# Two spectral and two dense layers on one core: the last two tiles of the first dense layer copied straight into the next layer's input, its last product in two column halves, and 38 idle products instead of 24

## The chip, the cores and the metric

The kernel runs on one core of a Trainium2 chip. The metric is device time in microseconds, the median of the runs of a kernel. The profile comes from one of these runs. Engines are named as the profile names them: PE (matrix products), PEld (loads of the stationary operand), DVE (vector), ACT (scalar and activation), POOL and SP. POOL, ACT and SP also issue DMA transfers, each on a queue of its own (q0, q10 and q1).

## The reference

`x` is 2048 tokens of 1024 features in bfloat16. Two kinds of layers are applied twice, each to a normalised `x` and added to `x`:

```
def _A_ref(x, w_r, w_i):                 # spectral filter
    X = rfft2(x.astype(float32)) * (w_r + 1j * w_i)
    return irfft2(X, s=(S, D)).astype(bfloat16)
def _B_ref(x, w1, b1, w2):               # dense, F = 3584
    h = x @ w1 + b1
    return (h * tanh(softplus(h))) @ w2  # mish
x = x + A(layernorm(x)); x = x + B(layernorm(x))
x = x + A(layernorm(x)); x = x + B(layernorm(x))
```

## The kernel before, in words

The four layers run one after another: `layer_A(0)`, `layer_B(0)`, `layer_A(1)`, `layer_B(1)`. The 2048 tokens are 16 tiles of 128, kept in `XS` (tile j in `XS[:, j, :]`). Both dense products use Winograd's form of a 2x2 block product with seven instead of eight block products. The order on every engine is the order in which the program records operations (`op`, `group`, `dma`); each engine runs its own list in order, and a semaphore wait is put in wherever one list needs another's result. A wait therefore holds up everything behind it on its engine or queue. Matrix products are recorded in groups, and one line (L1268 for the second dense product, L635 for the first step of the spectral layer) stands for all of them.

**The end of the first dense layer.** `products(1, ...)` computes the second dense product for tiles 8 to 15 in seven stages (`BACK`) of four token tiles t each. One `tile_product` is 14 products of 128x512 into one PSUM bank. Two sets of four banks alternate: `sets[0]` is banks 6, 7, 0, 1 and `sets[1]` is 2, 3, 4, 5. Stage 3 (`T2`) leaves its sum in `sets[1]`; stage 6 (`T4`) adds to those banks and yields the left 512 columns of tiles 12 to 15. `out` (L1319, DVE) adds bank, accumulator and `XS` into `XS`. `after` holds what is done with each stage's result. The accumulators `P1`, `X7` and `W` are float32 blocks of four tiles.

From stage 5 on, `extra` normalises each tile as soon as its left half is there: `stats_second` (DVE L562, then the aggregate L565), `root` (ACT L444, DVE L446), `apply` (DVE L524, into a ring of four buffers). The statistics of the right half were taken in stage 3.

**The way into the next layer.** The spectral layer's first step, `s1`, wants the tokens turned: `XR` has one partition per pair of tile and 128-column block, `row_of(j, h)`, and holds there 128 tokens x 128 features. A tile gets there in one of two ways. `xn_store` writes it to DRAM (`xn_scratch`, on POOL) and `xr_load` (on SP) reads it back as eight rows of 32 KB. `xr_direct` copies it from the ring buffer straight into the eight rows, one DMA per row and part. Tiles 0 to 14 go by DRAM; tile 15 goes directly in two parts of 64 tokens, that is 16 DMAs of 16 KB dealt over POOL, ACT and SP in turn. SP's list at this point is the loads of tiles 8 to 14, then its five direct copies; POOL's is the stores of tiles 8 to 14, six direct copies, and then the loads of the next layer's tables.

`s1` has 16 groups of eight products. Group j reads tokens 8j to 8j+7 of every tile, so groups 0 to 7 need the first half of all tiles and groups 8 to 15 the second half (`r_xr`). Each group fills a pair of banks, of which there are four, and is copied out by ACT (L641, groups 1, 3, 5, 7, 8, 9, 11, 13, 15) or DVE (L643). After `products` the kernel records `spin(24, 7)`: 24 products of 128x512 (L652) whose result in bank 7 nobody reads.

Of the kernel before, what the change touches and what calls it, by code (L numbers as in the profile page):

```python
# [6 lines left out]
ALU = mybir.AluOpType  # L7
P = 128
# [172 lines left out]
class KB:  # L181
# [375 lines left out]
    def stats_second(self, j, h, first):  # L557

        r = self.r_mv[j]
        if first:  # L560
            r.begin()
        self.op(self.dve, lambda e: e.bn_stats(self.BN[:, j, 6 * h:6 * h + 6], self.XS[:, j, 512 * h:512 * h + 512]),  # L562
                reads=[self.r_xs[j]], parts=[r])
        if not first:
            self.op(self.dve, lambda e: e.bn_aggr(self.MV[:, j, :], self.BN[:, j, :]), reads=[r], writes=[r])  # L565

    def pair(self):
        i = self.npair % 4
# [516 lines left out]
    def layer_B(self, li, last):  # L1085
        pe, dve, act, sp, pool = self.pe, self.dve, self.act, self.sp, self.pool
        PS, PSb, NF = self.PS, self.PSb, self.NF
# [174 lines left out]
            self.dma(pool, self.w2s_d[T_OF[name]][:, 7 * k:7 * k + 7, :], dst.ap, f"w2t{n}{k}", reads=[dst.res],  # L1262
                     writes=[self.r_w2d[T_OF[name]][k]])

        def tile_product(n, t, bank, ap, part, start):

            for k in range(2):
                self.group([lambda e, i=i, k=k, b=PB[n][k].ap: e.matmul(  # L1268
                    PS[:, bank, :], ap[:, i, t * P:(t + 1) * P], b[:, i - 7 * k, :],
                    start=(start and i == 0), stop=(i == 13), skip_group_check=True) for i in range(7 * k, 7 * k + 7)],  # L1270
                    reads=part(k) + [PB[n][k].res], writes=[self.r_bank[bank]])

# [3 lines left out]
        def products(p, s_off, stages, extra, loads=True):  # L1276
# [10 lines left out]
            ap = {"A11": AT[0][0].ap, "A12": AT[0][1].ap, "A21": AT[1][0].ap, "A22": AT[1][1].ap, "S": S.ap}  # L1287
# [10 lines left out]
            sets = ((6, 7, 0, 1), (2, 3, 4, 5))  # L1298
# [10 lines left out]
            def add(dst, bank, name, t):  # L1309
                (d, rd), (a, r) = acc(dst), acc(name)  # L1310
                self.op(dve, lambda e: e.tensor_tensor(d[t], PS[:, bank, :], a[t], ALU.add), reads=[self.r_bank[bank], r[t]], writes=[rd[t]])  # L1311

            def out(bank, name, t, i, h):
                x, rx = xs_of(i, t, h)
                a, reads = x, [self.r_bank[bank]]
                if name:
                    a, reads = acc(name)[0][t], reads + [acc(name)[1][t]]
                done = Res("done")
                self.op(dve, lambda e: e.tensor_tensor(x, PS[:, bank, :], a, ALU.add), reads=reads, writes=[rx, done])  # L1319
                if last:  # L1320
                    j = 4 * c[i] + t
                    self.dma(sp, self.out[0, j * P:(j + 1) * P, 512 * h:512 * h + 512], x, "st", reads=[done])
                elif stages is BACK and h:
                    self.stats_second(4 * c[i] + t, 1, True)

            def after(b, t, bank):

                if b == "B11":
                    a, r = acc("P1")
                    self.copy(act, a[t], PS[:, bank, :], [self.r_bank[bank]], [r[t]])  # L1330
                elif b == "B21" and stages is STD:
                    out(bank, None, t, 0, 0)
                elif b == "B21":
                    out(bank, "P1", t, 0, 0)
                elif b == "T3":
                    add("X7", bank, "P1", t)
                elif b == "T1":
                    add("W", bank, "X7", t)
                    fold("W", t, 1, 1)
                    if stages is BACK:  # L1340
                        fold("X7", t, 1, 0)
                elif b == "T2":
                    out(bank, "W", t, 1, 1)
                    add("W", bank, "P1", t)
                elif b == "B22":
                    fold("W", t, 0, 1)
                    out(bank, "W", t, 0, 1)
                    fold(*(("P1", t, 0, 0) if stages is BACK else ("X7", t, 1, 0)))
                else:
                    out(bank, "X7", t, 1, 0)  # L1350
# [6 lines left out]
            for n, (a, b, g, start) in enumerate(stages):  # L1357
                for t in range(4):
                    bank = sets[g][t]
                    if n or t:  # L1360
                        tile_product(n, t, bank, ap[a], lambda k: part(a, k), start)
                    after(b, t, bank)
                    for f, k in sums.get((n, t), ()):
                        f(k)
                    if t == 3 and n < 5 and loads:
                        for k in range(2):
                            load_b(stages, n + 2, k)
                    extra(n, t)
# [166 lines left out]
        def extra(n, t):  # L1535
            if n == 0:
                self.stats_act(12 + t)
            if not last:
                own_sums(n, t)
            if (n, t) == (1, 3):  # L1540
                self.sums_to_mv(12, 4)
                self.scales(12, 4)
                normal(12)
                for j in (13, 14, 15):
                    xn[j] = self.apply(j)
            if (n, t) == (2, 2):
                for j in (13, 14, 15):
                    transposed(3, j - 12, xn[j], act, (6, 7, 0)[j - 13])
            turn(2)
            if (n, t) == (4, 3) and not last:  # L1550
                ws[2:] = self.open_slots("WS", self.ob["WS"], 2)
                self.fill_slot(ws[2], 2)
            if n == 6 and not last:
                self.stats_act(t)
            if (n, t) == (5, 3):
                ws[0:2] = self.open_slots("WS", self.ob["WS"], 0, 1)
                for i in range(2):
                    self.fill_slot(ws[i], i)
                token_sums(1, last=False)
            if (n, t) == (6, 1):  # L1560
                B.update(token_sums(1))
# [26 lines left out]
        def extra(n, t):  # L1588
            if last:
                return  # L1590
            if (n, t) == (2, 0):
                self.warm(ACT.Sqrt)
            if (n, t) == (3, 3):
                self.open_xr()
                for j in range(8):
                    self.xr_load(j)
            if n >= 5:
                j = 4 * n - 12 + t
                self.stats_second(j, 0, False)
                self.root(j, 1)  # L1600
                b = self.apply(j, out=True)
                if j < 15:
                    self.xn_store(j, b)
                if j > 8:
                    self.xr_load(j - 1)
                if j == 15:
                    self.xr_direct(j, b, 2, (pool, act, sp))
        products(1, self.ob["XT2"], stages, extra)
        if not last:
            self.spin(24, 7)  # L1610


def build_kernel(nc, A_x, A_w_r, A_w_i, B_x, B_w1, B_b1, B_w2, out):
# [35 lines left out]
```

## Time and profile before

| what | value |
|---|---|
| median of 5 runs | 937.39 us (936.89 to 939.92) |
| profiled execution | 937.39 us, of which the span is 935.6 us |
| PE, share of the span busy | 94% |
| DVE, ACT, POOL | 66%, 46%, 17% |
| mean granted TensorE clock | 0.987 |
| last product of tile 15 read by DVE | 478.82 us |
| idle products | 478.62 to 483.96 us |
| first product of `s1` in the second spectral layer | 489.67 us |
| last copy out of `s1` ended | 501.04 us |

Times within the run count from the start of the span. A row of the timeline gives start, duration, engine, line, operation, output and inputs, and in brackets how long the engine had been idle and what ended that. Rows on SPq and ACTq are issues of DMAs; the transfer lands later. In the chain of waits every piece is what the next one waited for. "PEclk" in the table of windows is the granted clock as a part of full speed.

### The profile page before, as it was taken

The numbers are of one execution on the slowest core, as the hardware profiler recorded it, in microseconds if no ns is written. First come the engines' busy times: TensorE is split into PE (matmuls) and PEld (weight loads), VectorE is DVE, ScalarE is ACT, GpSimd is POOL, SyncE is SP. The second block draws the span as 40 slices with busy tenths as digits, with TensorE's granted clock in tenths as the row PEclk, the third lists the DMA queues.
The fourth block names the chain that finished last, engine by engine and source line by source line (L and its number), as shares of the span: only waits on it lengthen the run. The fifth ranks groups of instructions, "written<-read, shape, count | busy, mean of one in ns | idle before, by whom it ended". The sixth has DMA issues, their size and how long they took to land.

```text
span 935.6 us, 13481 instructions
## 1 busy us (share of the span) xinstructions
PE 876.5 (94%) x5473; PEld 472.1 (50%) x5473; DVE 618.9 (66%) x973; ACT 427.5 (46%) x623; POOL 159.1 (17%) x183
## 2 busy tenths in 40 slices
PE   0799799999999999999979987999999999999998
PEld 0577486444444444444437765754444444444443
DVE  7698368686889667568746865647746665554473
ACT  7798475456203475410008975745551015553000
POOL 3922003960004641010130200000000000000000
PEclk9999989999999999999999998999999999999999
DMA  9969854674786388364640798433155635832432
GB/s 287 259 232 300 202 134 122 216 277 142 262 262 243 138 311 292 115 243 143 251 147 32 221 228 200 159 118 119 54 185 177 209 113 190 282 118 74 175 125 112
DMA packets 146335, 174.68 MB, mean 187 GB/s; under 512 B 66248, under 2 KB 125736, under 8 KB 146152
## 3 DMA queue, kind: packets, MB, share of 16 engines
q1 hardware_dynamic: 133424, 127.48, 44.4%
q0 software_dynamic: 10672, 44.67, 13.3%
q10 hardware_dynamic: 2176, 1.66, 0.6%
q8 instruction: 43, 0.70, 0.3%
q14 instruction: 20, 0.16, 0.0%
HBM read 130.00 MB, written 40.89 MB: 183 GB/s over the span
## 4 chain that ended last, share of the span: by engine, by line
PE 81%; DMA 6%; DVE 5%; POOL 2%; ACT 2%; SPq 2%; issue 1%; DVEq 0%; POOLq 0%; ACTq 0%
PE PS L1268 35%; PE PS L1186 26%; PE PS L1148 9%; POOL ARENA L1081 2%; SPq L251 2%; PE PS L799 2%; PE PS L725 2%; PE PS L1020 2%; PE PS L824 2%; DMA ARENA<-in_B_w_dram 1%; PE PS L1109 1%; DMA ARENA<-in_A_x_dram 1%; DMA ARENA<-c_bt 1%; DMA ARENA<-u_scratch 1%; DMA u_scratch<-ARENA 1%
## 5 line engine op out<-in xcount | busy, mean ns | idle before, releaser
L1268 PE MATMUL PS<-ARENA 128*128 128x512 bf16 x1568 | 340.1, 379 | 0.0
L1186 PE MATMUL PS<-ARENA 128*128 128x512 f16 (+1 forms) x1232 | 267.8, 379 | 0.6 <-POOL ARENA L1081 0.5
L1268 PEld LDWEIGHTS PS<-ARENA 128*128 128x128 bf16 x1568 | 153.3, 98 | 184.6
L1191 DVE TENSOR_TENSOR ARENA<-PS,ARENA 128x512 f32<-128x512 f32 x220 | 151.8, 691 | 95.9 <-PE PS L1186 91.1
L1186 PEld LDWEIGHTS PS<-ARENA 128*128 128x128 bf16 x1232 | 120.2, 98 | 146.9 <-POOL ARENA L1081 2.5
L1196 ACT ACTIVATE ARENA<-ARENA,B 128x512 bf16<-128x512 f32 x132 | 95.1, 721 | 66.9 <-DVE ARENA L1191 60.8
L574 ACT ACTIVATE ARENA<-PS 128x512 f32<-128x512 f32 (+2 forms) x82 | 61.1, 745 | 119.4 <-PE PS L1186 96.4
L1148 PE MATMUL PS<-ARENA 128*128 128x256 bf16 (+1 forms) x576 | 87.4, 310 | 0.1
L1081 POOL TENSOR_TENSOR ARENA<-ARENA 128x512 bf16<-128x512 bf16 x56 | 71.3, 1273 | 74.7 <-DVE ARENA L524 60.1
L453 ACT ACTIVATE ARENA<-XS 128x1024 bf16<-128x1024 bf16 x52 | 54.8, 1053 | 36.9 <-DVE XS L1319 33.0
L1148 PEld LDWEIGHTS PS<-ARENA 128*128 128x128 bf16 x576 | 55.7, 99 | 26.7 <-DVE ARENA L1114 0.7
L1293 DVE TENSOR_TENSOR ARENA<-ARENA 128x3584 bf16<-128x3584 bf16 x32 | 63.9, 2017 | 0.0
L1319 DVE TENSOR_TENSOR XS<-PS,ARENA 128x512 bf16<-128x512 f32 x52 | 35.7, 689 | 39.0 <-PE PS L1268 38.7
L1152 ACT ACTIVATE ARENA<-PS,B 128x256 bf16<-128x256 f32 (+1 forms) x72 | 38.4, 541 | 35.8 <-PE PS L1148 35.3
L1311 DVE TENSOR_TENSOR ARENA<-PS,ARENA 128x512 f32<-128x512 f32 x48 | 32.9, 688 | 28.9 <-PE PS L1268 28.4
L1196 ACT ACTIVATE ARENA<-PS,B 128x512 bf16<-128x512 f32 x44 | 30.2, 685 | 18.0 <-PE PS L1186 18.0
L1307 DVE TENSOR_TENSOR ARENA<-ARENA,XS 128x512 f32<-128x512 f32 x52 | 36.7, 731 | 0.5
L1163 DVE TENSOR_TENSOR ARENA<-ARENA 128x2048 f16<-128x2048 bf16 x16 | 25.3, 1580 | 17.6 <-PE PS L1148 17.3
L799 PE MATMUL PS<-ARENA 128*128 128x256 bf16 x256 | 32.4, 273 | 3.9 <-DVE ARENA L788 3.2
L781 DVE TENSOR_TENSOR ARENA<-ARENA 128x1024 bf16<-128x1024 bf16 x32 | 22.0, 687 | 21.0 <-ACT ARENA L777 21.0
L472 DVE BATCH_NORM_STATS2 BN<-XS 128x6 f32<-128x512 bf16 x52 | 32.7, 671 | 4.6 <-DMA XS<-in_A_x_dram 4.6
L444 ACT ACTIVATE RS<-MV,EPS 128x1 f32<-128x1 f32 (+2 forms) x11 | 3.3, 296 | 70.7 <-DVE MV L565 70.0
(97 smaller groups left out, 832.5 us busy)
## 6 DMA issues: line engine op xcount, KB each, us to landing
ARENA<-in_B_w_dram SPq DMA_DIRECT2D x30, 896.0 KB, 6.5
ARENA<-w1s_scratch SPq DMA_DIRECT2D x30, 896.0 KB, 4.7
ARENA<-w2s_scratch SPq DMA_DIRECT2D x24, 896.0 KB, 6.6
ARENA<-in_B_w_dram SPq DMA_DIRECT2D x26, 512.0 KB, 5.3
w1s_scratch<-ARENA POOLq DMA_DIRECT2D x14, 896.0 KB, 4.2
u_scratch<-ARENA SPq DMA_DIRECT2D x14, 512.0 KB, 3.5
ARENA<-u_scratch SPq DMA_DIRECT2D x14, 512.0 KB, 5.9
w2s_scratch<-ARENA POOLq DMA_DIRECT2D x8, 896.0 KB, 4.2
```

The costliest lines, as they stand in the source:

```text
L453: self.op(act, lambda e, i=i, f=f: e.activation(junk.ap, x, f, accum_out=sums[:, i:i + 1]), reads=[self.r_xs[j]], writes=[junk.res], parts ...
L574: fn = (lambda e: e.activation(dst, src, ACT.Copy)) if scale is None else \
L799: fns.append(lambda e, c=c, part=part: e.matmul(ps[:, c * 256:(c + 1) * 256], yk.ap[:, part, c * P:(c + 1) * P], t[:, (128, 0)[part]:(384, ...
L1081: self.op(self.pool, lambda e, dst=A(dst), x=A(x), y=A(y), op=op: e.tensor_tensor(dst, x, y, op), reads=[b.res] + list(after), writes=[b.rs])
L1148: fns.append(lambda e, db=db, bank=bank, fl=fl: e.matmul(PS[:, bank, 0:w], wb.ap[:, db, fl * P:(fl + 1) * P], x.ap[:, db, tok], start=(db ...
L1152: self.op(act, lambda e, bank=bank, ft=ft, at=at: e.activation(at[:, tok], PS[:, bank, 0:w], ACT.Mish, bias=self.B1[:, ft:ft + 1]), reads= ...
L1186: self.group([lambda e, db=db: e.matmul(PS[:, bank, :], A[:, db, :], mov[:, db, :], start=(start and db == 0), stop=(db == 3), skip_group_ ...
L1191: self.op(dve, lambda e: e.tensor_tensor(dst.ap, PS[:, bank, :], x.ap, ALU.add), reads=[self.r_bank[bank], x.res], writes=[dst.res])
L1196: self.op(act, lambda e: e.activation(at, src, ACT.Mish, bias=self.B1[:, ft:ft + 1]), reads=[res, self.r_b1], writes=[ra])
L1268: self.group([lambda e, i=i, k=k, b=PB[n][k].ap: e.matmul(PS[:, bank, :], ap[:, i, t * P:(t + 1) * P], b[:, i - 7 * k, :], start=(start an ...
L1293: self.op(dve, lambda e: e.tensor_tensor(ap[dst][:, f, :], ap[x][:, f, :], ap[y][:, f, :], op), reads=part(x, k) + part(y, k), writes=part ...
L1307: self.op(dve, lambda e: e.tensor_tensor(a[t], a[t], x, ALU.add), reads=[rx], writes=[r[t]])
```

## The change

Tile 14 also goes directly, in one part: eight DMAs of 128 tokens x 128 features (32 KB), dealt alternately over POOL and SP; its store to DRAM and its load are gone, and the load of tile 13 stands on SP after SP's four copies. The 16 DMAs of tile 15 are dealt over the queues by a written list (ACT six, POOL six, SP four). The last product, stage 6 of tile 15, is computed as two halves of 256 columns. The left half goes on in its own bank; the right half starts anew in bank 1, and for that stage 3 adds its sum in these columns into `X7` beforehand. Each half is added into `XS` and gets its own statistics (`stats_columns`, four pieces of 256 columns and an aggregate over them, in the `BN` space of tiles 0 and 1). The idle products become 38.

```diff
+    def stats_columns(self, j, u):
+        r = self.r_mv[j]
+        if u == 0:
+            r.begin()
+        bn = self.BN[:, 0:2, :].rearrange("p a b -> p (a b)")
+        a = (512, 768, 0, 256)[u]
+        self.op(self.dve, lambda e: e.bn_stats(bn[:, 6 * u:6 * u + 6], self.XS[:, j, a:a + 256]), reads=[self.r_xs[j]],
+                writes=self.r_mv[0:2], parts=[r])
+        if u == 3:
+            self.op(self.dve, lambda e: e.bn_aggr(self.MV[:, j, :], bn), reads=[r] + self.r_mv[0:2], writes=[r])
...
-        def tile_product(n, t, bank, ap, part, start):
+        def tile_product(n, t, bank, ap, part, start, d=slice(0, 512)):
...
-                    PS[:, bank, :], ap[:, i, t * P:(t + 1) * P], b[:, i - 7 * k, :],
+                    PS[:, bank, d], ap[:, i, t * P:(t + 1) * P], b[:, i - 7 * k, d],
...
-            def out(bank, name, t, i, h):
+            def out(bank, name, t, i, h, d=slice(0, 512)):
...
+                elif stages is BACK and h and (i, t) == (1, 3):
+                    for u in range(2):
+                        self.stats_columns(15, u)
...
                 elif b == "T2":
                     out(bank, "W", t, 1, 1)
                     add("W", bank, "P1", t)
+                    if stages is BACK and t == 3:
+                        x7, r7 = acc("X7")
+                        self.op(dve, lambda e: e.tensor_tensor(x7[t][:, 256:512], PS[:, bank, 256:512], x7[t][:, 256:512], ALU.add),
+                                reads=[self.r_bank[bank]], writes=[r7[t]])
...
+                    if stages is BACK and (n, t) == (6, 3):
+                        for u, at in enumerate((bank, sets[0][t])):
+                            d = slice(256 * u, 256 * u + 256)
+                            tile_product(n, t, at, ap[a], lambda k: part(a, k), bool(u), d)
+                            out(at, "X7", t, 1, 0, d)
+                            self.stats_columns(15, 2 + u)
+                        extra(n, t)
+                        continue
...
-                self.stats_second(j, 0, False)
+                if j < 15:
+                    self.stats_second(j, 0, False)
                 self.root(j, 1)
                 b = self.apply(j, out=True)
-                if j < 15:
+                if j < 14:
                     self.xn_store(j, b)
-                if j > 8:
-                    self.xr_load(j - 1)
-                if j == 15:
-                    self.xr_direct(j, b, 2, (pool, act, sp))
+                    if j > 8:
+                        self.xr_load(j - 1)
+                elif j == 14:
+                    self.xr_direct(j, b, 1, (pool, sp))
+                    self.xr_load(13)
+                else:
+                    self.xr_direct(j, b, 2, (act, pool, sp, act, pool, act, pool, sp) * 2)
         products(1, self.ob["XT2"], stages, extra)
         if not last:
-            self.spin(24, 7)
+            self.spin(38, 7)
```

## The prediction

> **What bounds the kernel now**
>
> I read the page, the list of PE's waits, the chain of waits around the edited seam, the timeline there, the table of windows, and the DMA queues in short windows. PE is busy for 94% of the span, so the question is where it is not. PE's waits (what it waited for, total us, times, longest):
>
> ```profile
> PE PS L595 <- DVE ARENA L592: 21.2, 1, 21.2
> PE PS L1020 <- DMA ARENA<-u_scratch: 6.2, 4, 2.0
> PE PS L635 <- DMA ARENA<-ARENA: 5.7, 1, 5.7
> ```
>
> The first is the start of the kernel. The third is the longest single wait for a transfer, and the one place that the change touches. The chain of waits through it (start, us, what):
>
> ```profile
> 478.02 0.56 DVE ARENA L524
> 478.58 0.66 issue
> 479.24 2.84 DMA xn_scratch<-ARENA
> 482.08 0.02 issue
> 482.09 0.60 SPq L251
> 482.69 0.04 issue
> 482.74 0.54 SPq L251
> 483.28 0.04 issue
> 483.32 6.11 DMA ARENA<-ARENA
> 489.43 0.24 issue
> 489.67 4.82 PE PS L635 x48
> 494.49 0.02 issue
> 494.51 6.53 ACT ARENA L641 x7
> ```
>
> Tile 14 is normalised until 478.57, goes to DRAM and lands at 482.08. Only then can SP load it back, and SP's direct copies of tile 15 stand behind that load. The timeline shows that tile 15 itself was ready at 481.59, and that ACT and POOL began at once:
>
> ```profile
> 478.62 5.34 PE L652 MATMUL PS<-BD 128*128 128x512 bf16 x24
> 478.82 0.69 DVE L1319 TENSOR_TENSOR XS<-PS,ARENA 128x512 bf16<-128x512 f32 x1 [0.25 <-PE PS L1268]
> 481.04 0.55 DVE L524 TENSOR_SCALAR ARENA<-XS,MV,RS 128x1024 bf16<-128x1024 bf16 x1
> 481.62 3.35 ACTq L251 DMA_DIRECT2D ARENA<-ARENA  x5
> 482.74 3.17 SPq L251 DMA_DIRECT2D ARENA<-ARENA  x5
> ```
>
> The windows (length, busy PE, PEld, DVE, ACT, POOL, then PEclk, DMA share, GB/s) show a second loss. The idle products end at 483.96, the clock halves about 3.1 us later and stays half for 6.6 us:
>
> ```profile
> 487.10:489.60 2.50, 0.00 (x0) 0.00 (x0) 0.00 (x0) 0.00 (x0) 0.00 (x0) 0.50 0.48 76
> 489.60:493.70 4.10, 4.03 (x39) 4.06 (x40) 2.45 (x2) 1.44 (x2) 0.00 (x0) 0.50 0.00 0
> ```
>
> At half clock PE sets the pace of s1: its first copies out start 0.85 us apart (490.72, 491.58, 492.43, 493.28). From 494.51 ACT copies without a gap, so there ACT does.
>
> Why do SP's copies take up to 6 us? SP's queue in the 0.1 us from 482.70, when the load of tile 13 moves (packets, MB, share of 16 engines):
>
> ```profile
> q1 hardware_dynamic: 8, 0.26, 1024.5%
> ```
>
> Eight packets of 32 KB take 10.245 x 1.6 = 16.4 us of engine time, or 2.05 us each on eight engines. Load 14 then runs from about 484.5 on the same eight, and whatever is queued there waits: the last 40 packets of SP's direct copies move at 488.1 to 489.4. I read these two as one cause; the trace does not name the engines.
>
> **The change, part by part**
>
> *Tile 14 directly.* Removed: POOL's store of tile 14 (0.89 us of issue, 2.84 to landing) and SP's reload (0.60 of issue, eight packets of 2 us). Added: eight copies of 32 KB, four on POOL at about 0.54 us and four on SP at about 0.60 (the medians of the direct copies' issue). SP starts at 478.6 and is through by 481.1. The reload of tile 13 now stands behind these four, but it waits anyway for its store, which landed so that it issued at 481.33. So SP is free at about 481.9 for tile 15, against 482.74. POOL is through by about 481.4, before tile 15 is ready. New in flight on the eight slow engines at 480.6 to 481.7 are the direct packets, beside the rest of store 13: 4 copies x 9 packets x about 22 ns (SP's copies at 487 to 488) = 0.8 us at most, so load 13 moves between 482.75 and 483.5 and is done at 484.8 to 485.5. There is no load 14 behind it.
>
> *Order of queues for tile 15.* ACT gets six copies instead of five, SP four instead of five, three ACT, three POOL and two SP in each half. The first half is issued by about 483.7, and needs 1.4 us to its first packets (ACT's issue at 481.62, packets at 483.0). Packets on the eight engines flush after load 13: the eight copies of a half are 8 x 80 packets over 16 engines, 40 each at about 25 ns, so 1 us. The first half and tile 13 are there at 486.0 to 487.2. Copies of the second half leave by 485.8; they gate the ninth group of s1, over 4 us after its start, and cost nothing. POOL's FT table load keeps its place at 485.1.
>
> *More idle products.* 24 took 5.34 us, or 0.2157 us each more. 38 starting at 478.65 end at 487.0. So s1 starts at the later of 487.0 and the data: I take 487.1, **2.57 us earlier than 489.67**. The spin itself may hold it up by up to 1 us; if the data are late it costs nothing.
>
> *Clock.* The wait after the idle products falls from 5.7 us to a few tenths, and the clock should stay full. Then s1 is set by ACT's nine copies (groups 1, 3, 5, 7, 8, 9, 11, 13, 15): a group of eight takes 0.64 us alone (first layer's s1 in the chain of waits), the second is there at about 1.0 us, then 2 x 1.02 + 7 x 0.93 = 8.55, in all 9.6 us. Before, s1 took from 489.67 to 501.04 = 11.37. **Gain 1.77 us.** DVE's seven copies of 1.2 us fit beside it.
> Rule and row: the Trainium skill, "TensorE: Matmul & The Clock Gate" (Terms, and "What's actually happening"), gives one idle window of about 3.4 us to the half clock, and a price of throttled time x (1 - K/N). On the whole 6.6 us this makes 3.3 us and the sum 931.8; but products ran for only 4.0 us of it, which makes 2.0 and 933.1. I keep 1.77, since at full clock the copies take over as the limit.
>
> *Last product in halves.* PE: 28 products of 256 columns at 0.109 us (L1148's eight in 0.87) are 3.05 us for 3.02. The second half goes to a free bank, so PE waits for no read. On DVE the intended gain, a shorter last add and statistics (0.69 + 0.69), is not there: DVE is busy with tile 14 until 478.57, and waits only 0.25 us for the full product today. After that come two adds (estimate 0.42 each[...]) and two statistics (0.413, the 256-column row L484), 1.8 us with gaps against 1.70 now, and an aggregate of 24 values (0.264) instead of 12 (0.209). Tile 15 is ready **0.15 to 0.2 us later**, at 481.77. ACT's first copies move with it, but the spin's end covers that.
>
> *Stage T2.* One more add of 0.42 us and two statistics of 256 for one of 512 (+0.14). Both come with the stage's last tile (add at 443.89), after which DVE idles 0.83 us before the add of 446.00; hidden there, and 0.56 us outright if that gap were gone.
>
> *Later.* Everything behind s1 moves 4.3 us earlier. In the lull of the next stage the clock is half from 572.7 to 579.1. In the first layer the same lull was half for 10 us, and the way from its start to the long products took 24.30 us (114.78 to 139.08) against 23.25 (570.93 to 594.18). Where the clock's window falls is new after the shift: between -0.2 and +1.05 us, I take +0.3.
>
> A rule speaks against the change: the Trainium skill, "DMA: Bandwidth & Descriptors" (Anatomy of one DMA; Bandwidth), gives about 2.0 us fixed per transfer and calls transfers under 64 KB descriptor-dominated. Taken one after another, four of 32 KB on SP are 4 x 2.08 = 8.3 us from 478.6: load 13 would leave at 487, arrive at 491, and s1 would start at about 492, a loss of 2.6 us. The rows say that transfers in one queue overlap: ACT's copies, issued 0.6 to 0.75 us apart, move packets at that same pitch. I go with the rows.
>
> Sum: 2.57 + 1.77 - 0.3 = 4.0 us. The profiled execution took 937.39 us, of which 935.6 is span, and is the median of the five, so the time is **933.3 us**.
>
> **Rivals**
>
> 1. *Data late, clock kept.* Load 13 or a queue is later than I think, and s1 starts between 488 and 490. With idle products until 487.0 the wait stays under 3.1 us. For: store 13 shares engines with the new copies, and landings of up to 6.1 us have been seen. Against: no load 14. Gain 1.77 + (0 to 1.7) - 0.3: 934.2 to 935.9.
> 2. *Small copies clog SP's queue; slower.* SP's four copies of tile 14 stand ahead of load 13 and of SP's part of tile 15. If each 128-row copy held the queue for the 2 us of the rule or more, s1 starts at 492 or later. Past 490.1 (487.0 + 3.1) the clock halves again and the gain of 1.77 is gone too, so this is the point from which it decides. Start at 492 to 494: 2.3 to 4.3 us slower, 939.7 to 941.7. For: ACT's landings are on average 1.5 us apart where issues are 0.7. Against: those landings fall together with the 32 KB packets, and packets elsewhere follow the issues.
> 3. *The seam's gain is given back.* The next lull in the half clock for the longer time (-1.05), and the spin or s1's copies slower than I count: about 935.5 to 937.
>
> **How the numbers follow**
>
> My forecast 0.67, with 932.0 to 934.5 as its own range; rival 1 0.16, rival 2 0.09, rival 3 0.08. A run of this kernel tells 0.2%, 1.87 us, from no change: the borders are 935.52 and 939.26. Faster: 0.67 + 0.12 of rival 1 + 0.03 of rival 3 = 0.82. Slower: 0.08 of rival 2. Same: the rest, 0.10. The range goes from 931.8 (data early, s1 on ACT alone) to 936.2, which leaves out rival 2 and half of rival 3.
>
> **What would show it right or wrong**
>
> In the changed kernel: 38 idle products ending near 487; s1's first product within about 1 us after them; granted clock 1.00 over all of s1; ACT's copies out of s1 without gaps, s1 about 9.6 us long; aggregate of tile 15 at about 480.4 (no gain from the halves); SP's reload of tile 13 still near 481.3 to 482.1; no store and load of tile 14. I am wrong if s1's wait for a direct copy is again over 3 us, if the clock is half at s1's start, or if tile 15 is normalised clearly before 481.5.

## The result and the profile after

| | before | after |
|---|---|---|
| median | 938.35 us (48 runs) | 936.25 us (27 runs, 933.02 to 940.85) |
| ratio | | 0.9981, 95% interval 0.9971 to 0.999 |
| profiled execution | 937.39 us, span 935.6 us | 935.05 us, span 933.2 us |
| mean granted clock in it | 0.987 | 0.993 |

About half of the forecast gain: 2.1 us (938.35 less 936.25) for 4.1 (937.39 less 933.3), and just outside the range, which ended at 936.2. The forecast started from a median of five runs, 937.39; 48 runs of the same kernel gave 938.35. Two further measurements of the unchanged kernel after gave 935.62 and 937.57 us; the interval of the second reaches no change (table below).

The chain of waits of the kernel after through the seam (start, us, what):

```profile
476.86 5.77 DMA xn_scratch<-ARENA
...
482.64 0.66 SPq L251
...
483.90 4.65 DMA ARENA<-ARENA
488.56 0.26 issue
488.82 0.62 PE PS L647 x8
...
492.98 5.61 ACT ARENA L653 x6
```

It is the chain of before, one tile earlier: the store of tile 13, SP's load of tile 13, one of SP's copies of tile 15, `s1`. That last copy took 4.65 us (6.11 before). A queue's copies of one half report to one semaphore, so this is the time until all of SP's first half was reported. PE's wait for it was 1.1 us. The timeline:

```profile
479.36 8.37 PE L664 MATMUL PS<-BD 128*128 128x512 bf16 x38
488.82 6.83 PE L647 MATMUL PS<-M,ARENA 128*128 128x128 bf16 x104 [1.09 <-DMA ARENA<-ARENA]
489.91 8.68 ACT L653 ACTIVATE ARENA<-PS 128x1024 bf16<-128x1024 f32 x9 [8.29 <-PE PS L647]
```

The short wait flatters: the idle products now end at 487.73 instead of 483.96, so most of the old wait lies under them. What counts is `s1`'s first product, at 488.82 against 489.67. ACT's nine copies run without a gap, because the clock stayed full, as the windows show (the columns as before):

```profile
487.10:489.60 2.50, 1.41 (x18) 0.91 (x16) 0.14 (x1) 0.00 (x0) 0.00 (x0) 1.00 0.47 89
489.60:493.70 4.10, 3.97 (x66) 3.48 (x64) 4.10 (x4) 3.68 (x4) 0.00 (x0) 1.00 0.00 0
```

The way up to the seam differs by up to 1.5 us from profile to profile, so seams are compared from DVE's read of tile 14's last product, here called out 14: 475.80 before, 476.50 after. From there `s1` starts at +13.87 before and +12.32 after, and its last copy ends at +25.24 and +22.09. That is 3.15 us in these two profiles: 1.55 in the start, 1.60 in the length of `s1` (11.37 and 9.77). Of it, 0.70 is taken off because this run reached out 14 later (the other two profiles of the same kernel reached it at 475.50 and 475.15, so the change is not the reason), and 2.45 is left, against 2.4 between the spans. From the end of `s1` to the end of the span it is 434.56 us before and 434.61 after: nothing was given back there.

### The profile page after: what moved, and what is told of

Read it like the earlier page. It is cut to its first block, busy times and chain, and to the rows that moved or that the text cites. A ratio compares the mean times of both kernels' runs of the same rounds, so it can differ in the third digit from the quotient of the medians.

```text
span 933.2 us, 13549 instructions
## 1 busy us (share of the span) xinstructions
PE 878.2 (94%) x5501; PEld 472.8 (51%) x5501; DVE 619.7 (66%) x977; ACT 427.6 (46%) x623; POOL 159.8 (17%) x186
## 4 chain that ended last, share of the span: by engine, by line
PE 81%; DMA 6%; DVE 6%; POOL 3%; ACT 2%; issue 1%; SPq 1%; POOLq 0%; DVEq 0%; ACTq 0%
PE PS L1280 34%; PE PS L1198 26%; PE PS L1160 9%; POOL ARENA L1093 2%; PE PS L811 2%; PE PS L737 2%; PE PS L836 2%; PE PS L1032 2%; DMA XS<-in_A_x_dram 1%; DMA ARENA<-in_B_w_dram 1%; PE PS L1121 1%; DMA ARENA<-c_bt 1%; DMA ARENA<-u_scratch 1%; POOL ARENA L251 1%; DVE ARENA L655 1%; DMA u_scratch<-ARENA 1%
## 5 line engine op out<-in xcount | busy, mean ns | idle before, releaser
L1280 PE MATMUL PS<-ARENA 128*128 128x512 bf16 (+1 forms) x1582 | 340.1, 377 | 0.0
L1331 DVE TENSOR_TENSOR XS<-PS,ARENA 128x512 bf16<-128x512 f32 (+1 forms) x53 | 35.8, 679 | 38.2 <-PE PS L1280 38.0
L789 ACT ACTIVATE ARENA<-PS 128x1024 bf16<-128x1024 f32 x32 | 33.4, 1075 | 4.5 <-PE PS L785 4.5
```

The source lines that it names most:

```text
L1280: self.group([lambda e, i=i, k=k, b=PB[n][k].ap: e.matmul(PS[:, bank, d], ap[:, i, t * P:(t + 1) * P], b[:, i - 7 * k, d], start=(start an ...
```

## The experiments

Times in the table count from out 14; "long" is from the first product of `s1` to its last copy; the clock is that during the wait and `s1`. The median of before in the five batches was 937.85, 938.1, 938.46, 938.61 and 938.69 us.

| run | median us | ratio to before [95%] | first product of s1 | PE's wait | s1 long | clock |
|---|---|---|---|---|---|---|
| before (profile) | 938.35 | | +13.87 | 5.7 | 11.37 | half, 7 us |
| after (profile) | 936.25 | 0.9981 [0.9971, 0.999] | +12.32 | 1.1 | 9.77 | full |
| e1_direct14 | 937.88 | 0.9996 [0.9984, 1.0008] | +13.49 | 5.3 | 10.75 | half, 3.5 us |
| e2_spin38 | 937.5 | 0.9988 [0.9977, 0.9999] | +14.46 | 3.3 | 12.12 | half, 7 us |
| e3_nohalves | 937.09 | 0.9985 [0.9972, 0.9997] | +13.53 | 2.3 | 11.02 | half, 3.5 us |
| e4_after | 935.62 | 0.9975 [0.9963, 0.9987] | +13.32 | 2.1 | 9.77 | full |
| e6_direct13 | 937.92 | 0.9998 [0.9988, 1.0007] | +14.71 | 3.5 | 10.76 | half, 3.5 us |
| e7_direct13_spin30 | 938.31 | 1.0003 [0.9992, 1.0014] | +15.14 | 5.6 | 11.34 | half, 7 us |
| e8_ftlate | 936.04 | 0.9981 [0.9973, 0.9989] | +12.73 | 1.5 | 9.77 | full |
| e10_spin44 | 935.69 | 0.9972 [0.9962, 0.9982] | +14.63 | 2.1 | 11.01 | half, 3.5 us |
| e11_no13 | 936.03 | 0.9976 [0.9964, 0.9987] | +12.72 | 3.2 | 12.05 | half, 7 us |
| e12_15only | 931.91 | 0.9935 [0.9923, 0.9947] | +10.18 | 0.7 | 9.77 | full |
| e13_alldirect | 940.43 | 1.002 [1.0007, 1.0033] | +16.39 | 6.5 | 11.46 | half, 7 us |
| e14_alldirect_spin30 | 940.84 | 1.0024 [1.0013, 1.0035] | +17.57 | 8.1 | 11.13 | half, 7 us |
| e15_14and15 | 935.36 | 0.9969 [0.9957, 0.9981] | +12.04 | 2.5 | 11.00 | half, 3.5 us |
| e16_13and15 | 934.94 | 0.9962 [0.9951, 0.9974] | +12.07 | 2.6 | 9.77 | full |
| e17_onepart | 937.06 | 0.999 [0.9978, 1.0001] | +13.64 | 2.4 | 11.03 | half, 3.5 us |
| e18_actstore | 934.67 | 0.9963 [0.995, 0.9975] | +13.13 | 1.9 | 9.76 | full |
| e19_actstore44 | 934.36 | 0.9958 [0.994, 0.9976] | +13.02 | 0.5 | 9.77 | full |
| e20_after | 937.57 | 0.9987 [0.9973, 1.0001] | +14.54 | 3.3 | 9.76 | full |

**The parts of the change.** e1_direct14 is before with tile 14 sent directly and the new dealing of the queues; e2_spin38 is before with more idle products; e3_nohalves has both and lacks the column halves; e4_after is the whole change again.

```diff
+                elif j == 14:                                          # e1, e3
+                    self.xr_direct(j, b, 1, (pool, sp))
+                    self.xr_load(13)
...
-            self.spin(24, 7)
+            self.spin(38, 7)                                           # e2, e3
```

> The kernel before with the direct copies of tile 14 and the new deal of queues alone (24 idle products, no halves). Theory (two gains that need each other): s1 starts about 1.5 us earlier than before counted from DVE's read of tile 14's last product (13.87 us there), since the reload of tile 13 now gates it; the idle products still end 5 us after the last product, PE then waits over 4 us, so the clock is half at s1's start and s1 takes about 11.4 us. Sum: 1.5 us faster, ratio 0.998. Rival (the clock is the whole gain): no change, ratio 1.000. Rival (the idle time is now short enough to keep the clock): 3 us faster.

> The kernel before with 38 idle products alone. Theory: s1 starts 13.9 us after DVE's read of tile 14's last product as before, the wait after the idle products falls from 5.7 to 2.7 us. If the clock halves only after 3.1 us of idling, s1 is at full clock and takes 9.7 instead of 11.4 us: 1.6 us faster, ratio 0.9983. Rival (the clock is judged in fixed windows of about 3.4 us, so it depends on where the wait falls): half of the runs gain, the median moves by under 1 us and the runs spread over 2 us more. Rival (the clock was no part of the gain): ratio 1.000.

> The changed kernel without the column halves: direct copies of tile 14, new deal of queues, 38 idle products. Theory (halves bring nothing, since DVE is busy with tile 14 when the last product ends): same as the changed kernel within 0.2 us, tile 15 normalised 5.8 us after DVE's read of tile 14's last product against 5.9 with halves; ratio to before 0.998. Rival (halves are what brings tile 15 earlier): slower than the changed kernel by 0.5 us.

> The changed kernel once more, for a second profile beside the others on one chip. Theory: from DVE's read of tile 14's last product to the end of s1 it is 22.1 us at full clock, against 25.2 before, so 3.1 us faster at the seam; the median gains less (about 2 us) because in some runs the clock halves at s1 or longer in the lull behind it, which would show as a granted clock under 0.99 in the slow runs. Rival (the direct copies land late in some runs): slow runs with a clock of 0.993 and an s1 that starts over 13 us after that read.

Measured: each part alone is within 0.12% of before. With tile 14 direct and 24 idle products PE still waits 5.3 us and the clock goes; with 38 idle products alone the data come at +14.46, the wait is 3.3 us and the clock goes too. Together they bring 0.15 to 0.25% (e3, e4); these intervals overlap that of e2 (0.9977 to 0.9999), so how the gain divides is not settled by the medians. With e1 the first product came at +13.49, not near the forecast +11.3 nor the 1.5 us expected of this run: the direct way of tile 14 is itself worth only some tenths. The halves cost DVE 0.1 us, as forecast: tile 15 is normalised at +5.90 with them (e4_after) and +5.80 without (e3_nohalves). Their own effect on the time isn't told apart: the intervals of e3_nohalves and e4_after overlap.

**What might hold the copies of tile 15.** e6_direct13 and e7_direct13_spin30 send tile 13 directly as well, so that the last reload is tile 12's; e8_ftlate holds back a table load of POOL (`c_ft`, 192 KB) that moves between the copies; e10_spin44 has 44 idle products.

```diff
+                elif j == 13:                                          # e6, e7
+                    self.xr_direct(j, b, 1, (pool, sp))
+                    self.xr_load(12)
...
+        late = [self.Y.res] if self.li and g == 2 else []              # e8: c_ft waits for s1's result
...
+            self.spin(44, 7)                                           # e10
```

> The changed kernel with tile 13 also copied directly (eight copies of 128 rows, four on POOL and four on SP, before SP's reload of tile 12), still 38 idle products. Theory (the reload of tile 13, with its 32 KB rows on eight DMA engines, holds the direct copies back): data are ready before the idle products end, PE waits under 0.2 us for a transfer, s1 starts 11.3 us after DVE's read of tile 14's last product (12.3 and 13.3 in the two profiles of the changed kernel), the clock stays full in every run: 1 to 2 us faster than the changed kernel, ratio 0.996. Rival (the FT table load on POOL is what holds them back): s1 starts at 12.3 to 13.3 as in the changed kernel, no gain. Rival (more small copies clog SP's queue): s1 later than 13.3, slower than the changed kernel.

> As e6_direct13 with 30 idle products, which end 9.6 us after the same read. Theory: data are ready at 10 to 10.7, so s1 starts there, 0.6 to 1.3 us earlier than in e6_direct13, at full clock; ratio 0.995. Rival (FT table load): s1 at 12.3 to 13.3 after 3 us of idling, the clock halves, ratio 0.999 or more.

> The changed kernel with the third FT table's load (POOL, right behind its direct copies) held until s1 is done, where it still has 4 us before its use. Theory (reload of tile 13): s1's start moves by under 0.3 us. Rival (the table's packets from DRAM delay the last packets of the direct copies on the engines they share): s1 starts 0.8 to 1.5 us earlier, about 11.5 to 12 us after the read, and the median is 1 us or more under the changed kernel's. Both may hold in part: then about 0.5 us.

> The changed kernel with 44 idle products, which end 12.6 us after the read. Theory (in part of the runs the wait between the idle products and s1 lets the clock halve, so the changed kernel's runs spread from 933 to 941): the wait falls under 0.8 us, the slow runs go, the median falls by 1 us or more against the changed kernel and no run has a granted clock under 0.988. Rival (the spread has other causes): same spread, and a median 0 to 0.3 us worse.

Measured: one more direct tile makes the start later, +14.71 and +15.14. Without the table in the way `s1` starts at +12.73, inside the spread of the kernel after (+12.32 to +14.54 in three profiles), and the time is that of after, so the table is at most a small part of it. With 44 idle products the data were late too (+14.63; tile 13's store had needed 7.6 us to land), and the clock was lost in the middle of `s1`; the time, 935.69 us, is within the spread of after, and its runs still reach from 932.2 to 940.2 us, which they were expected not to do.

**Leaving tiles out.** In the next kernels a tile's rows of `XR` are filled early with those of a tile that was stored long before (j - 8), and its own store, load or copies are left out, so the next layer works on that tile's values in its place; 30 idle products make the landing visible as PE's wait. e11_no13 leaves out tile 13, e12_15only tiles 13 and 14. e13_alldirect, and e14_alldirect_spin30 with 30 idle products, are complete kernels with tiles 8 to 15 direct.

```diff
+                self.xr_load(13, 5)                                    # e11, e12, e15: rows of tile 13 from tile 5
+                self.xr_load(14, 6)                                    # e12, e16: rows of tile 14 from tile 6
+                self.xr_load(12, 4)                                    # e15: rows of tile 12 from tile 4
...
-                if j < 14:                                             # e13, e14
-                    self.xn_store(j, b)
-                    if j > 8:
-                        self.xr_load(j - 1)
-                elif j == 14:
+                if j < 15:
+                    b.unread = False
                     self.xr_direct(j, b, 1, (pool, sp))
-                    self.xr_load(13)
```

> The kernel after with tile 13's store and reload left out of the seam: its rows of s1's input are filled early from tile 5's (so tile 13's values in the output are tile 5's in effect), and 30 idle products instead of 38 (end near 485.3). Times are counted from the read of tile 14's last product (out 14). Theory A (the store, reload and eight 32 KB rows of tile 13 pin s1's start, because the copies of tile 15 queue behind them on SP and on eight DMA engines): s1 starts at +10.0 to +11.3 and the clock stays full, 934.0 to 935.0. Rival B (the small copies of tiles 14 and 15 land late by themselves): s1 starts at +12.3 to +13.5, as in the kernel after, with 2 to 3 us of waiting, 935.5 to 937.

> As the kernel without tile 13 at the seam, and tile 14's direct copies left out too (its rows filled early from tile 6's), so that only tile 15's sixteen copies remain at the end; 30 idle products. Theory A: little more to gain, s1 at +9.7 to +10.8, within 0.8 us of the kernel without tile 13. Rival B1 (tile 14's eight copies delay tile 15's): s1 over 1 us earlier than without tile 13 alone. Rival B2 (tile 15's own copies take 5 us to land after they are issued): s1 still at +12 or later, so nothing gained by leaving out either.

> The kernel after with tiles 8 to 13 also sent directly (eight copies each, POOL and SP in turn), so no store, no reload and no 32 KB row in the last eight tiles; 38 idle products as before. Theory A: every tile's copies are through before the next one is ready, so s1 starts at the end of the idle products, about +11.0 to +11.6, clock full, 934.3 to 935.5. Rival B (small copies are slow to land and pile up: 48 more of them, and POOL or SP fall behind): s1 at +12.3 to +15, 935.6 to 938.

> The same with 30 idle products, which end near 485.3 at +9.6, so that the landing of tile 15's first half itself is seen as PE's wait. Theory A: s1 at +10 to +11.3 with a wait under 1.5 us, 933.8 to 935.3. Rival B: s1 no earlier than with 38, a wait of 3 us or more and the clock at half in part of s1, 936.5 to 938.

Measured: without tile 13 little or nothing is gained (+12.72), which spoke against my reading, that the 32 KB rows are the cause. Without tile 14 as well `s1` starts at +10.18 and the time falls to 931.91 us. The chain of waits of e12_15only:

```profile
482.25 0.86 ACTq L251
483.11 0.03 issue
483.14 2.30 DMA ARENA<-ARENA
485.44 0.49 issue
485.92 0.62 PE PS L648 x8
```

This is what tile 15 needs when tiles 13 and 14 are out of the way: 2.3 us from issue to landing, half of the 4.65 in the kernel after. All tiles direct is slower than before. The table of DMAs of e12_15only and then of e13_alldirect (output and input, queue, count, size, median us from issue to landing):

```profile
ARENA<-ARENA ACTq DMA_DIRECT2D x6, 16.0 KB, 2.4
ARENA<-ARENA POOLq DMA_DIRECT2D x6, 16.0 KB, 2.1
ARENA<-ARENA SPq DMA_DIRECT2D x4, 16.0 KB, 2.2
```

```profile
ARENA<-ARENA ACTq DMA_DIRECT2D x6, 16.0 KB, 6.5
ARENA<-ARENA POOLq DMA_DIRECT2D x6, 16.0 KB, 6.0
ARENA<-ARENA SPq DMA_DIRECT2D x4, 16.0 KB, 7.1
```

The windows of e13_alldirect point to why (the last three columns are the clock, the mean share of 16 DMA engines, GB/s):

```profile
480.00:484.00 4.00, 4.00 (x20) 1.84 (x19) 2.58 (x7) 0.29 (x1) 2.82 (x7) 1.00 1.22 68
484.00:488.00 4.00, 3.08 (x15) 1.18 (x12) 0.00 (x0) 0.00 (x0) 3.15 (x6) 1.00 1.54 64
```

The engines have packets open all the time (the shares add up to over 1, so packets overlap in this count), and still only 64 to 68 GB/s move. A tile of 262,144 bytes needs 3.9 to 4.1 us at that pace, and a tile is ready every 3.02 us (out 14 to the next one, 475.80 to 478.82 before): they pile up, as the rival had it. The time of one packet, from packets and share in one us, first of e12_15only at 483, then of e13_alldirect at 485:

```profile
q10 hardware_dynamic: 160, 0.03, 15.0%
```

```profile
q1 hardware_dynamic: 237, 0.05, 124.7%
```

0.150 x 16 us over 160 packets is 15 ns; 1.247 x 16 over 237 is 84 ns. There the same small packet takes over five times as long. The late copies also hold up DVE, which waits for a buffer that they still read: in e14_alldirect_spin30 tile 15 itself is ready 1.3 us later than in after (+7.15 for +5.90).

**Rows or small copies.** Both suspects were still in e11_no13, since load 12's rows had moved into the place of load 13's. So e15_14and15 leaves out tiles 12 and 13 (no 32 KB row moves near the end), and e16_13and15 leaves out tile 14 only. e17_onepart is the kernel after with tile 15 in eight copies of 128 tokens, e18_actstore has the stores of tiles 8 to 13 on ACT's queue.

```diff
+                    self.xr_direct(j, b, 1, (act, pool, sp, act, pool, act, pool, sp))     # e17, tile 15
...
+        prog, tag = (self.act, "xa") if j >= 8 else (self.pool, "xw")                      # e18, e19: xn_store
```

> The rows of tiles 12 and 13 are left out of the seam (filled early from tiles 4 and 5), so that no 32 KB row moves after about 477; tile 14 and tile 15 go directly, 30 idle products. Counted from out 14. Theory P (the small copies of tile 14 and tile 15 slow each other: packets take 15 ns alone and 30 to 80 when many copies are open): s1 at +12 to +13, as without tile 13, about 935.5 to 936.5. Theory R (32 KB rows of whatever tile comes last hold eight engines for 2 us, and without tile 13 it was load 12's): s1 at +10 to +10.8, as with tile 15 alone, about 932 to 933.5.

> Tile 14 is left out of the seam (its rows filled early from tile 6's), tile 13 still goes by store and reload, tile 15 directly; 30 idle products. Theory P: without tile 14's small copies s1 starts at +10.2 to +11, about 932 to 933.5. Theory R: load 13's rows and SP's queue behind it still hold tile 15's copies, s1 at +12 to +13.5, about 935.5 to 937. Both causes together would show +12 in both of these kernels.

> The kernel after with tile 15 copied in one part (eight copies of 128 rows, issued in half the time) instead of two: half as many copies, but s1's start now needs all of tile 15. 38 idle products. Theory P: the packets are the same and the last of the tile lands as late as it did (c. 489 to 490), so s1 is 0.5 to 1.5 us later than in the kernel after (+13.5 to +14.5) and the clock is lost more often: 936.5 to 938. Rival (the number of copies counts, each with its own fixed cost): s1 at +11.5 to +12.5 and 934.5 to 935.5, better than after.

> The kernel after with the stores of tiles 8 to 13 on ACT's queue (ACT idles for most of this stage) instead of POOL's. Store 13 is issued at once and load 13 needs not wait for 5.5 to 8 us. Theory R: load 13 leaves 0.5 to 2 us earlier, SP's copies of tile 15 with it, s1 at +11.3 to +12.3, 934.5 to 935.5. Theory P: store 13's landing is set by the packets ahead of it on the engines, whichever queue it comes from; s1 stays at +12.3 to +14, 935.5 to 936.5.

Measured: +12.04 and +12.07 where tile 15 alone had +10.18. Each of the two, tile 14's small copies without any 32 KB row, and tile 13's rows without tile 14, costs 1.9 us by itself in these profiles. One profile stands for each, and three of the kernel after lie 2.2 us apart, so the size is rough; that each costs something the medians show: 935.36 and 934.94 us against 931.91, with intervals far apart. The chain of waits of e15_14and15:

```profile
480.76 0.81 ACTq L251
...
481.60 4.23 DMA ARENA<-ARENA
485.83 0.45 issue
```

The same third copy of ACT as in e12_15only, issued just as soon after tile 15, lands after 4.23 instead of 2.30 us. Its packets are not slower and not late. ACT's queue up to 483.25 in e15_14and15 and up to 484.75 in e12_15only, 1.6 us after that copy's issue in both (481.60, 483.14):

```profile
q10 hardware_dynamic: 240, 0.05, 10.4%
```

```profile
q10 hardware_dynamic: 240, 0.05, 6.0%
```

In both all 240 packets of the three copies (480 for the six) have begun by then, at 15 to 16 ns each (0.104 x 16 x 2.25 us and 0.060 x 16 x 3.75 us over 240). The landing comes at 485.83 and 485.44, that is 2.6 and 0.7 us later. So what tile 14's copies delay here is the report of the landing, behind the packets. And of e16_13and15:

```profile
477.25 5.63 DMA xn_scratch<-ARENA
...
482.90 0.60 SPq L251
...
483.55 0.61 SPq L251
...
484.21 4.52 DMA ARENA<-ARENA
488.73 0.24 issue
488.97 0.62 PE PS L648 x8
```

Here SP waits for the store of tile 13 (5.63 us), issues the load, and then its copies of tile 15. SP's queue in the us from 484:

```profile
q1 hardware_dynamic: 8, 0.26, 104.5%
```

1.045 x 16 us over eight packets is 2.1 us each, as before the change. It is not SP's queue alone that they delay. The last copies of the first half on each queue, in e16_13and15:

```profile
ARENA<-ARENA ACTq DMA_DIRECT2D x1, 16.0 KB, 4.5
ARENA<-ARENA SPq DMA_DIRECT2D x1, 16.0 KB, 4.5
ARENA<-ARENA POOLq DMA_DIRECT2D x1, 16.0 KB, 4.1
```

With both in place the nine profiles that have them (e1, e3, e8, e10, e18, e19 and the three of after) start `s1` at +12.32 to +14.63, on average +13.4: later than with one, by less than the sum. Tile 15 in one part gave +13.64, which is inside that spread: half as many copies, with all of the tile needed at once, bring nothing; the two effects are not told apart. With the stores on ACT's queue load 13 left at +5.32 (e18) and +6.99 (e19), the store having landed 5.1 and 7.2 us after its issue, for 5.2 to 7.8 us in the three of after: no sooner from this queue.

**A better version.** e19_actstore44 has both, the stores on ACT's queue and 44 idle products; e20_after is the kernel after beside it.

> The stores of tiles 8 to 13 on ACT's queue and 44 idle products. If the two add up (s1 starts no earlier than the data allow, but the clock is never lost at the seam), 934.0 to 935.0 and below the kernel after in the same batch by about 1 us; if the lower time of the run with ACT's stores was the clock's lull in the second layer alone, the same as the kernel after, 935.5 to 936.3.

> The kernel after once more, unchanged, beside the one above: 935.6 to 936.5, s1 at +12.3 to +13.5 from the read of tile 14's last product.

The timeline of e19_actstore44, with idle products up to 0.51 us before the data are there:

```profile
478.93 9.66 PE L665 MATMUL PS<-BD 128*128 128x512 bf16 x44
489.09 6.83 PE L648 MATMUL PS<-M,ARENA 128*128 128x128 bf16 x104 [0.51 <-DMA ARENA<-ARENA]
```

It is 934.36 us (seven runs, of which the one profiled is the longest) against 937.57 for after beside it, 0.9958 and 0.9987 of before, with intervals that still touch (0.994 to 0.9976, and 0.9973 to 1.0001). It has the lowest median of the complete kernels, and e18_actstore points the same way (934.67); that it is better is likely, not shown. Why is not settled: `s1` starts no earlier (+13.02, +13.13), and its length is that of after.

## Why the prediction was right or wrong

**The start of `s1`: the step that failed.** The prediction put it at 487.1, which is +11.3, a gain of 2.57 us. Measured: +13.4 on average where before and e2_spin38, the two profiles of the old way, have +13.87 and +14.46, a gain of 0.8 us (rough, as the nine spread over 2.3 us). What failed is "The first half and tile 13 are there at 486.0 to 487.2", which is +10.2 to +11.4: in the kernel after they were there at 488.55, +12.05. Two terms of it were too small.
- *The packets.* It counted 40 packets an engine at 25 ns, from the us at 487 of the trace of before, and set tile 14's copies at "0.8 us at most", for four of the eight. By e15_14and15 against e12_15only those copies cost 1.9 us. The packets themselves went about as counted; what has no term in the sum is the time from a copy's last packet to the report of its landing, 0.7 us in e12_15only and 2.6 in e15_14and15. In the kernel after SP's and ACT's queues (q1, q10) had begun all packets of both halves of tile 15 but one by 487.50, and the first half was reported at 488.55. The queues from 487.50 to 491:

```profile
q0 software_dynamic: 52, 0.14, 15.2%
q10 hardware_dynamic: 1, 0.00, 0.0%
```

What the report waits for is not shown. Slower packets, as the 84 ns of e13_alldirect, are not it in e15_14and15.
- *The load of tile 13.* "There is no load 14 behind it" was right, but one load is enough: 1.9 us by e16_13and15 against e12_15only. Load 13 was issued at +6.14 in the kernel after (forecast +5.5 to +6.3), and its rows moved at about the old price (2.3 us each, 2.05 before), in the half us from 483.76:

```profile
q1 hardware_dynamic: 8, 0.26, 227.6%
```

Here too the last copies of the first half land alike on all three queues:

```profile
ARENA<-ARENA ACTq DMA_DIRECT2D x1, 16.0 KB, 4.7
ARENA<-ARENA SPq DMA_DIRECT2D x1, 16.0 KB, 4.7
ARENA<-ARENA POOLq DMA_DIRECT2D x1, 16.0 KB, 4.3
```

`s1` starts 6.2 us after load 13's issue (482.64 to 488.82), where the forecast allowed 5.0 to 5.8 (487.1 less 482.1 and 481.3). In e20_after the load left at +8.12 and `s1` followed 6.4 us later. The load's time is not the only limit: in e4_after it left at +5.53, `s1` started 7.8 us later, and ACT's copy was the last.

The prediction read landings of 6 us in before as one cause, the rows. The trace did not name the engines, it said so, and went on as if it did. The rule that it set aside spoke of small transfers as costly; the estimate from it, one copy after another, was 492, and that did not happen either. The fixed time of a copy alone agrees with it (2.1 to 2.4 us in e12_15only, on all three queues, for about 2.0, which its page gives for copies issued by POOL); what other copies under way add is not in it.

**The clock: right in size, not in certainty.** Whenever the clock stayed full, `s1` was 9.76 to 9.77 us long, in eight profiles (9.6 forecast), so 1.60 us shorter than before for 1.77; the 2.0 us that the Trainium skill's rule gave is further off. But the wait does not stay at "a few tenths": 1.1, 2.1 and 3.3 us in the three profiles of after. The clock stayed full in those, and was lost in e3_nohalves and e10_spin44 with waits of 2.3 and 2.1. Over all runs the time at half clock (twice the missing clock times the span) is about 24 us before and 18 us after, and within before and within after the time rises by 0.24 and 0.29 us with each us of it. 6 x 0.27 is 1.6 us, so by this estimate most of what was measured is the clock's; it rests on runs that differ by chance, and late data lengthen a run and lose the clock at once.

**The halves:** no gain, 0.1 us later (0.15 to 0.2 forecast); an add of 256 columns took 0.42 us, as estimated. **Stage T2:** hidden, as forecast. DVE's new add fills the pause of 0.83 us, and the next read of a product comes no later than it did:

```profile
445.39 0.41 DVE L1362 TENSOR_TENSOR ARENA<-PS,ARENA 128x256 f32<-128x256 f32 x1
445.72 0.68 DVE L1319 TENSOR_TENSOR ARENA<-ARENA,XS 128x512 f32<-128x512 f32 x1
446.43 0.69 DVE L1331 TENSOR_TENSOR XS<-PS,ARENA 128x512 bf16<-128x512 f32 x1
```

From the stage's last add into `XS` to out 14 it is 33.24 us in both (442.56 to 475.80, 443.26 to 476.50).

**The next lull** (0.3 us lost, forecast): between 0 and 1.3. From the end of `s1` to the end of the span it is 434.61 us in the kernel after, with 7 us of half clock in that lull, and 435.81 and 435.85 in e4_after and e20_after, with 10 us. Kernels without the whole change show both too (434.56 before, 435.83 in e1_direct14), so these few profiles give no reason to put it down to the change.

**Sum.** 0.8 + 1.6 = 2.4 us before any loss in the lull, for 2.1 measured; the 0.1 us of the halves is already in the start. The missing 1.8 us of 2.57 is the failed step. Of the rivals the first came true, "data late, clock kept", with the start at 488.82 where it said 488 to 490; the time is 0.35 us above its upper end. The second did not: SP was through with tile 14's copies at 481.78 (479.30 + 2.48) and had to wait for the store of tile 13 anyway. Its price did appear elsewhere, in e13_alldirect: with 56 such copies in place of 8 the kernel is slower than before. The third gave a range that holds the measured time (935.5 to 937), but not in its way: in the kernel after nothing was given back in the lull, in e4_after and e20_after 1.2 us was, as in e1_direct14.

## What to carry to other kernels

Here a copy that goes round a store and a reload saved their latency for itself and delayed the copies behind it: before sending one more tile directly, ask what is queued behind it and leave it out altogether in one run, which shows the most that can be won (here 6.5 us, of which 2 were had). A copy's landing time read in a quiet moment (2.3 us) was half of that in a crowded one (4.2 to 4.7), and counting packets did not show it: take the time to the landing, not to the last packet. Idle products that should keep the clock and copies that bring the data sooner act on the same wait, so judge such edits together.

## What the runs showed of the hardware that I had not expected

*The length of the wait does not decide whether the clock is lost.* The timeline and windows of e20_after: 3.31 us of waiting, clock full throughout.

```profile
489.69 6.83 PE L647 MATMUL PS<-M,ARENA 128*128 128x128 bf16 x104 [3.31 <-DMA ARENA<-ARENA]
```

```profile
487.00:489.00 2.00, 0.00 (x0) 0.00 (x0) 0.00 (x0) 0.00 (x0) 0.00 (x0) 1.00 0.31 71
489.00:491.00 2.00, 1.31 (x24) 1.34 (x25) 0.67 (x1) 0.22 (x1) 0.00 (x0) 1.00 0.00 0
```

And of e10_spin44: 2.11 us of waiting, and the clock goes 1.2 us after `s1` has begun, for 3.5 us.

```profile
490.83 8.01 PE L647 MATMUL PS<-M,ARENA 128*128 128x128 bf16 x104 [2.11 <-DMA ARENA<-ARENA]
```

```profile
490.20:492.00 1.80, 1.17 (x22) 1.21 (x23) 0.53 (x1) 0.08 (x1) 0.00 (x0) 1.00 0.00 0
492.00:495.50 3.50, 3.50 (x38) 3.50 (x36) 3.05 (x3) 2.48 (x3) 0.00 (x0) 0.52 0.00 0
```

The half-clock stretches at the seam are about 3.5 or 7 us long. That agrees with the fixed, free-running window of 3.4 us of which the Trainium skill speaks ("TensorE: Matmul & The Clock Gate", What's actually happening), by which what falls into one window would count, not the pause. That a whole window must be idle is not borne out by e10_spin44, where PE was busy for part of any 3.4 us around the wait.

*A small copy's price depends on its company:* 2.1 to 2.4 us to landing alone, 6.0 to 7.1 with a crowd, and 64 to 68 GB/s at full queues. In e15_14and15 landings are later although no long row is about, and the delay lies between the last packet and the report (2.6 us for 0.7). The Trainium skill ("DMA: Bandwidth & Descriptors", Queues, rings and completion order) says that the write that reports a landing comes only after every earlier write of that DMA engine, across its queues. That would couple the copies in this way, and all three queues alike; the traces do not name the engines, so no run here isolates it.
